# Seven products of block sums for the first MLP from token 768 on, its weights streamed from memory

## The chip, the cores and the metric

The program runs on one core of one Trainium2 chip. The metric is the device time of one execution in microseconds (us). The engines are named as the profile names them: PE (TensorE, matrix products), PEld (its weight loads), DVE (VectorE), ACT (ScalarE), POOL (GpSimd) and SP (SyncE, here the only queue that issues transfers).

## What is computed

The reference is windowed attention followed by two MLPs. There are 4 sequences of 576 tokens, 8 heads of 64, so 2304 tokens of width 512:

```
scores = q @ k.T / sqrt(64), masked: heads 0-3 see the 32 last positions,
         heads 4-7 every 4th of the 128 last positions
x  = softmax(scores) @ v                      # 2304 x 512
h  = x @ moe_w_in;   x  = relu(h)**2 @ moe_w_out      # 512 -> 2048 -> 512
h  = x @ moe2_w_in;  y  = silu(h)    @ moe2_w_out
```

The weights arrive as 64-bit floats. The kernel turns them into 32-bit values and splits each into a high and a low part; each product of the MLPs is made of three matmuls (high x high, high x low, low x high).

## The kernel before

**Order.** Nothing is scheduled by hand. Every piece of work is an `op` with the engines that may run it, a duration for each, its dependencies and a key. `Planner.order` builds the whole order before the launch: it takes again and again the operation that can start first (a key counts 0.005 us per unit, so keys only decide between near ties), and writes it to the program of its engine. A `gate` holds a transfer back until the first MLP or the second has come to a given key. One key unit stands for one 128-wide slice of the hidden layer on a 256-token tile. All transfers stand in one in-order queue, SP's.

**Buffers.** `POOLS` has 28 pages of 1024 words per partition ("u4"), 8 of 512 ("u2") and 2 of 512 ("u3"). `HOLDS` says which uses share a pool and `MOST` how many pages each use may hold. The converted first weights of MLP 1 (`w0`) hold 16 pages of u4, one for each of 16 slices, until the last token tile has used them. The second weights of the running MLP lie in 16 buffers of their own (`w1`).

**Attention.** 32 blocks: 8 halves of sequences (h, 288 tokens each) by 4 pairs of heads. A block is scores on PE, mask and row minimum on DVE (L572), exponential on ACT (L577), normalisation (L581 to L593), transpose (L600), product with v (L622), and then a cast into x's high part and a subtraction for its low part, for each 256-token tile that the block touches.

**First MLP** (`mlp`). Nine tiles of 256 tokens. The first three run interleaved, because their matmuls wait for weights that are still being converted and for attention; the other six follow one by one. For each slice c: S1 is 12 matmuls (L686 to L688), then max and square (L702, L710), cast and subtraction (L360, L367), then S2 is 12 matmuls (L734 to L736). The result goes to DRAM as `y1`.

**Second MLP** (`mlp2`). Four tiles of 512 tokens and one of 256. For a 512-token tile two slices (a pair) form a 2 x 2 block product, and S1 is done with seven products of block sums instead of eight: 42 matmuls of 256 columns for a pair (L832). Five additions put the blocks together (L846, L848). S2 has 24 matmuls of 512 columns for a pair (L881 to L883). The weights and their block sums are streamed for each tile from DRAM, where they were stored after conversion (`w2s`, `w2x`); `load_x2` reads `y1` back and makes the block sums of x (L799).

**Weights of the second MLP.** `weights(1, c, ...)` converts both halves of chunk c while MLP 1 runs, and stores them to `w2s`; `sums` makes block sums of the first half and stores them to `w2x`; `fetch` reads the second half back into `w1` during the last tile of MLP 1.

Of the kernel before, what the change touches and what calls it, by code (L numbers as in the profile page):

```python
# [23 lines left out]
P = 128  # L24
# [9 lines left out]
TILES = ([(t, 256) for t in range(0, NT, 256)], [(0, 512), (512, 512), (1024, 512), (1536, 512), (2048, 256)])  # L34

POOLS = {"u4": (28, 1024), "u2": (8, 512), "u3": (2, 512)}
HOLDS = {"w0": "u4", "wa": "u4", "ws": "u4", "wb": "u4", "wc": "u2", "h": "u4", "raw": "u4", "ap": "u4", "x": "u4", "x2": "u4", "g4": "u4", "st": "u4",
# [264 lines left out]
def c_dma(nbytes):  # L302
    return nbytes / 250e3
# [6 lines left out]
class Kern:  # L310
# [59 lines left out]
    def weights(self, m, c, key, dkey):  # L370
# [3 lines left out]
        for j in range(2):  # L374
            raw = self.spot("raw", n, I64)
            cv = self.spot("cv", n)
            both = (self.spot("st", 2 * n, F32R) if m else self.spot("w0", 2 * n, F32R) if j == 0 else
# [5 lines left out]
            k = key + (1.5 if m else 0.5) * j  # L383
# [3 lines left out]
                           [], dkey + (1.5 if m else 0.5) * j, [raw], name=f"R{at}")  # L387
            if m:
                load.gate = dkey + 1.5 * j
# [36 lines left out]
            if m:  # L426
                self.kept[c, j] = self.op({"DMA": c_dma(P * n * 8)}, lambda e, both=both, c=c, j=j: nc.sync.dma_start(
                    out=self.w2s[c, j], in_=both.tile.bitcast(F32)), [h, r], k, [], [both])
# [7 lines left out]
    def sums(self, f, key):  # L436

        nc = self.nc
        (ca, wa), (cb, wb) = self.cv[2 * f], self.cv[2 * f + 1]
# [7 lines left out]
        for i, (x, y, op) in enumerate(what):  # L447
# [5 lines left out]
                                + ([s[0]] if i == 3 else []), f"S{f}.{i}", True))  # L453
        self.kept[f, "s"] = []
        for i in range(2):
            hi, lo = Part(s[i], 0, PIECE), Part(s[i], PIECE, PIECE)
            h = self.op({"ACT": c_act(PIECE), "Pool": c_pool1(PIECE)}, lambda e, hi=hi, lo=lo: self.copy(
                e, hi.tile, self.f32(lo)), [done[2 * i], done[2 * i + 1]], key, [], [s[i]], f"h1.{f}.s{i}")
            deps = [h] + ([done[3]] if i == 0 else [])
            r = self.op({"DVE": c_dve(PIECE), "Pool": c_pool2(PIECE)}, lambda e, hi=hi, lo=lo: self.sub(  # L460
                e, lo.tile, self.f32(lo), hi.tile.bitcast(F32)), deps, key, [], [s[i]], f"l1.{f}.s{i}", True)
            self.kept[f, "s"].append(self.op({"DMA": c_dma(P * PIECE * 8)}, lambda e, i=i: nc.sync.dma_start(
                out=self.w2x[f, i], in_=s[i].tile.bitcast(F32)), [h, r], key, [], [s[i]]))
# [6 lines left out]
    def fetch(self, c, key):  # L470

        nc = self.nc
        both = self.buf("w1", NF, 2 * PIECE, F32R)
        o = self.op({"DMA": c_get(P * PIECE * 8)}, lambda e: nc.sync.dma_start(
            out=both.tile.bitcast(F32), in_=self.w2s[c, 1]), [self.kept[c, 1]], key, [both])
        o.gate = key
        self.wt[1, 1, c] = (Part(both, 0, PIECE), Part(both, PIECE, PIECE), o, o)

    def stream(self, f, key, whole):
# [4 lines left out]
        def load(use, src, n, deps, i):  # L484
            b = self.spot(use, n, F32R)
            o = self.op({"DMA": c_get(P * n * 4)}, lambda e: nc.sync.dma_start(
                out=b.tile.bitcast(F32), in_=src), deps, key + i, [b])
# [3 lines left out]
        b, o = load("wa", self.w2s[2 * f, 0], 1024, [self.kept[2 * f, 0]], 0)  # L491
        out["a11"], out["a12"] = [(Part(b, i, 256), Part(b, 512 + i, 256), o) for i in (0, 256)]
        n = 512 if whole else 1024
        b, o = load("wc" if whole else "wb", self.w2s[2 * f + 1, 0, :, :n], n, [self.kept[2 * f + 1, 0]], 0.1)
# [3 lines left out]
        else:  # L498
            for j in range(2):
                b, o = load("ws", self.w2x[f, j], 1024, [self.kept[f, "s"][j]], 0.2 + j)  # L500
# [28 lines left out]
    def attention(self, h, pair, key, step):  # L529
# [100 lines left out]
        for t in range(h * HALF // 256, (h * HALF + HALF - 1) // 256 + 1):  # L630
            lo, hi = max(h * HALF, t * 256), min(h * HALF + HALF, t * 256 + 256)
# [7 lines left out]
            def dst(b, t=t, lo=lo, hi=hi):  # L639
                o = b.tile[:, lo - t * 256:hi - t * 256]  # L640
                return o.rearrange("p (s r) -> p r s", r=DIL) if dil else o

            def src(lo=lo, hi=hi):
                if dil:
                    return xb.tile[:, :HALF].rearrange("p (r s) -> p r s", r=DIL)[
                        :, :, (lo - h * HALF) // DIL:(hi - h * HALF) // DIL]
                return xb.tile[:, lo - h * HALF:hi - h * HALF]

            w = hi - lo
# [104 lines left out]
    def load_x2(self, t, key):  # L754

        nc = self.nc
        t0, n = TILES[1][t]
        raw, got = [], []
        for j in range(2):
            b = self.buf("blk", BLK_BUFS, BLK_COLS)  # L760
            raw.append(b)
            for i in range(2):
                k = 2 * j + i
                deps = [self.ydone[0, u, k] for u, (u0, un) in enumerate(TILES[0]) if u0 < t0 + n and t0 < u0 + un]
                d = self.op({"DMA": c_dma(P * n * 4)}, lambda e, k=k, i=i, b=b: nc.sync.dma_start(
                    out=b.tile[:, n * i:n * i + n], in_=self.y1[k][:, t0:t0 + n]), deps, key + k, [] if i else [b], [b] if i else [])
                d.gate = key - 8
                got.append(d)
        x = self.x[1, t] = {}
# [5 lines left out]
        def keep(name, key, src, deps, uses):  # L775
# [5 lines left out]
                        [b], uses, f"xh{t}.{name}")  # L781
            r = self.op({"Pool": c_pool2(512), "DVE": c_dve(512)}, lambda e: self.sub(e, v(lo), src(), v(hi).bitcast(F32)),
                        [h], key + 0.1, [], uses + [b], f"xl{t}.{name}", True)
# [14 lines left out]
        for i, (p, q, uses, deps, of) in enumerate(what):  # L798
            done.append(self.op({"Pool": c_pool2(512), "DVE": c_dve(512)}, lambda e, i=i, p=p, q=q: self.eng[e].tensor_tensor(  # L799
                out=at(i), in0=p(), in1=q(), op=ALU.subtract), list(deps) + ([] if of is None else [done[of]]),  # L800
                key + 5 + i, [sums[i]], list(uses) + ([] if of is None else [sums[of]]), f"xs{t}.{i}", True))
            keep(("t1", "t2", "t4", "t3")[i], key + 5.5 + i, lambda i=i: at(i), [done[i]], [sums[i]])

    def mlp2(self, t, k0, fetched):

        nc = self.nc
        t0, n = TILES[1][t]
        x = self.x[1, t]
# [162 lines left out]


W_KEY = 4.0
A_LEAD = 22.0
B_LEAD = 6.0
A1 = -5.0
A2 = 6.0
# [93 lines left out]
```

## Time and profile before

| | |
|---|---|
| time, median of 3 runs | 919.78 us (919.67 to 920.01) |
| the profiled execution's own time | 919.36 us |
| its span, first to last instruction | 917.6 us |
| PE, PEld busy | 908.1 us (99%), 853.0 us (93%) |
| DVE, ACT, POOL busy | 588.1 us (64%), 466.6 us (51%), 66.9 us (7%) |
| transfers | 167.67 MB, 183 GB/s over the span |

The span is what the profile shows; the execution's time is 1.76 us longer. Busy shares are averages over stages that are limited by different things, so the rows further down are cut by stage. Matmuls overlap in the records (each is listed with 280 ns and more but the next starts after some 120 ns), so the pace is read from start to start.

### The profile page before, as it was taken

Reading aid. Unit: us, or ns where it says so; the run is one execution under the profiler, and the core shown is the slowest. Engines: PE = TensorE matmul, PEld = TensorE weight load, DVE = VectorE, ACT = ScalarE, POOL = GpSimd, SP = SyncE. Lnnn points to the kernel's source line nnn. Section 1 sums busy time; section 2 is a strip of 40 time slices with the busy share of each in tenths; the row PEclk is TensorE's granted clock in tenths of the full one; section 3 lists DMA queues with packets and bytes.
Section 4 is the critical chain, followed back from the end, with each engine's and each line's share of the span. In section 5 each row is a group of like instructions: output and inputs, shape, how many; then the busy total and the mean of one; then the engine's idle time right before and its main releaser. Section 6 shows DMA issues by size and latency. Waiting matters only on the chain.

```text
span 917.6 us, 19481 instructions
## 1 busy us (share of the span) xinstructions
PE 908.1 (99%) x7325; PEld 853.0 (93%) x7325; DVE 588.1 (64%) x1711; ACT 466.6 (51%) x1374; POOL 66.9 (7%) x83
## 2 busy tenths in 40 slices
PE   8999999999999999999999999999999999999998
PEld 7889999998999999999999999999999899999998
DVE  6999993478998988885522357466448454444422
ACT  7978772578877787775423234234224222322222
POOL 2224200001010111210000000000000000000000
PEclk9999999999999999999999999999999999999999
DMA  8356330147767586663004987556565657545150
GB/s 322 96 192 236 139 108 1 33 156 249 253 236 263 196 255 240 218 227 138 25 1 148 348 301 281 185 205 226 171 211 179 236 167 257 215 153 168 39 207 24
DMA packets 55390, 167.67 MB, mean 183 GB/s; under 512 B 6144, under 2 KB 12032, under 8 KB 55296
## 3 DMA queue, kind: packets, MB, share of 16 engines
q1 hardware_dynamic: 55296, 166.42, 52.7%
q8 instruction: 58, 0.95, 0.4%
q14 instruction: 36, 0.29, 0.1%
HBM read 131.79 MB, written 34.60 MB: 181 GB/s over the span
## 4 chain that ended last, share of the span: by engine, by line
PE 90%; DVE 5%; ACT 3%; issue 1%; POOL 0%; ACTq 0%; DVEq 0%
PE s L832 20%; PE s L686 7%; PE y L881 7%; PE y L882 7%; PE y L883 7%; PE s L688 7%; PE s L687 7%; PE y L734 7%; PE y L735 6%; PE y L736 6%; PE ax L550 2%; PE ax L622 1%; PE ax L600 1%; ACT ap L577 1%; DVE ap L593 1%; PE zx L734 1%
## 5 line engine op out<-in xcount | busy, mean ns | idle before, releaser
L686 PE MATMUL s<-x,w 128*128 128x256 f32 x576 | 166.2, 289 | 0.7 <-ACT ap L360 0.5
L688 PE MATMUL s<-x,w 128*128 128x256 f32 x576 | 162.7, 282 | 0.2 <-DVE w L367 0.2
L687 PE MATMUL s<-x,w 128*128 128x256 f32 x576 | 162.2, 282 | 0.0
L848 DVE TENSOR_TENSOR h<-s,h 128x512 f32<-128x512 f32 (+1 forms) x128 | 79.9, 624 | 113.3 <-PE s L832 112.0
L734 PE MATMUL y<-g,w 128*128 128x256 f32 x512 | 147.7, 289 | 0.0
L735 PE MATMUL y<-g,w 128*128 128x256 f32 x512 | 144.3, 282 | 0.1
L736 PE MATMUL y<-g,w 128*128 128x256 f32 x512 | 144.2, 282 | 0.0
L367 DVE TENSOR_TENSOR g<-r,g 128x256 fp32r<-128x256 f32 (+1 forms) x220 | 109.4, 509 | 36.2 <-ACT g L360 32.3
L360 ACT CAST g<-r 128x256 fp32r<-128x256 f32 (+1 forms) x224 | 103.6, 466 | 45.6 <-DVE r L710 27.2
L881 PE MATMUL y<-g,w 128*128 128x512 f32 (+1 forms) x320 | 118.0, 369 | 0.0
L882 PE MATMUL y<-g,w 128*128 128x512 f32 (+1 forms) x320 | 117.8, 368 | 0.0
L883 PE MATMUL y<-g,w 128*128 128x512 f32 (+1 forms) x320 | 117.7, 368 | 0.0
L710 DVE SCALAR_TENSOR_TENSOR r<-s,r 128x256 f32<-128x256 f32 x144 | 60.5, 420 | 86.8 <-ACT r L702 85.4
L686 PEld LDWEIGHTS s<-x,w 128*128 128x128 f32 x576 | 109.1, 189 | 4.4 <-ACT ap L360 0.7
L702 ACT ACTIVATE r<-s 128x256 f32<-128x256 f32 x144 | 54.7, 380 | 109.3 <-PE s L688 96.1
L688 PEld LDWEIGHTS s<-x,w 128*128 128x128 f32 x576 | 109.3, 190 | 0.5 <-DVE w L367 0.4
L687 PEld LDWEIGHTS s<-x,w 128*128 128x128 f32 x576 | 109.4, 190 | 0.0
L867 ACT ACTIVATE r<-h 128x512 f32<-128x512 f32 x64 | 37.0, 625 | 133.6 <-DVE h L848 133.6
L734 PEld LDWEIGHTS y<-g,w 128*128 128x128 f32 x512 | 96.8, 189 | 1.4
L832 PE MATMUL s<-x,ws 128*128 128x256 f32 x768 | 97.5, 283 | 0.0
L735 PEld LDWEIGHTS y<-g,w 128*128 128x128 f32 x512 | 96.6, 189 | 0.4 <-DVE g L367 0.3
L736 PEld LDWEIGHTS y<-g,w 128*128 128x128 f32 x512 | 96.4, 188 | 0.0
(90 smaller groups left out, 1610.8 us busy)
## 6 DMA issues: line engine op xcount, KB each, us to landing
raw<-w SPq DMA_DIRECT2D x64, 512.0 KB, 5.2
ws<-w2x SPq DMA_DIRECT2D x64, 512.0 KB, 4.4
wa<-w2s SPq DMA_DIRECT2D x40, 512.0 KB, 4.3
w2s<-st SPq DMA_DIRECT2D x32, 512.0 KB, 3.1
w2x<-st SPq DMA_DIRECT2D x16, 512.0 KB, 3.3
w<-w2s SPq DMA_DIRECT2D x16, 512.0 KB, 4.9
wc<-w2s SPq DMA_DIRECT2D x32, 256.0 KB, 4.6
blk<-qkv SPq DMA_DIRECT2D x8, 608.0 KB, 4.1
```

Of the source, the lines that this page charges most:

```text
L360: self.nc.scalar.copy(out=out, in_=in_)
L367: self.eng[eng].tensor_tensor(out=out, in0=a, in1=b, op=ALU.subtract)
L686: nc.tensor.matmul(o, wh.tile[:, s], xh, start=(kk == 0), stop=False)
L687: nc.tensor.matmul(o, wh.tile[:, s], xl, start=False, stop=False)
L688: nc.tensor.matmul(o, wl.tile[:, s], xh, start=False, stop=(kk == KC - 1))
L734: nc.tensor.matmul(o, wh.tile[:, s], gh.tile, start=(c == 0 and o0 == 0), stop=False, **kw)
L735: nc.tensor.matmul(o, wh.tile[:, s], gl.tile, start=False, stop=False, **kw)
L736: nc.tensor.matmul(o, wl.tile[:, s], gh.tile, start=False, stop=(c == NF - 1), **kw)
L832: nc.tensor.matmul(bank.tile[:, o:o + 256], wp, xp, start=i == 0, stop=last, skip_group_check=True)
L881: nc.tensor.matmul(o, wh.tile[:, s], gh.tile, start=c == 0, stop=False)
L882: nc.tensor.matmul(o, wh.tile[:, s], gl.tile, start=False, stop=False)
L883: nc.tensor.matmul(o, wl.tile[:, s], gh.tile, start=False, stop=(c == NF - 1))
```

## The change

Tiles of MLP 1 become 3 of 256 tokens and 3 of 512. The three large ones run through `mlp2`, which is generalised to both MLPs (for MLP 1 the two-step sigmoid product is replaced by one max-and-square instruction on DVE). Their first weights come by `stream(0, ...)` from DRAM: each converted chunk of `w0` is also stored (`w1s`), and `sums(f, key, 0)` adds high and low part of two chunks back together (`cw`), makes four block sums, splits and stores them (`w1x`). The attention output of tokens from 768 on is copied once (`xo`), stored to DRAM (`x1`), and read and split by `load_x`. The second half of MLP 2's weights is no longer converted during MLP 1's middle, stored and fetched: it is loaded and converted straight into `w1` during MLP 1's last tile. Keys, the transfer cost in the planner's table and a few hints move too.

```diff
-TILES = ([(t, 256) for t in range(0, NT, 256)], [(0, 512), ...
+TILES = ([(0, 256), (256, 256), (512, 256), (768, 512), (1280, 512), (1792, 512)], [(0, 512), ...
-    return nbytes / 250e3          # c_dma, the planner's cost of a transfer
+    return nbytes / 330e3
...
             else:
                 self.wt[m, j, c] = (hi, lo, h, r)
+                if m == j == 0:
+                    self.kept[0, c] = self.op({"DMA": ...}, ... nc.sync.dma_start(
+                        out=self.w1s[c], in_=both.tile.bitcast(F32)), [h, r], k + W1_BACK, [], [both])
...
+        if m == 0:                                   # sums
+            for c in (2 * f, 2 * f + 1):
+                b = self.spot("cw", PIECE)
+                wh, wl, h, l = self.wt[0, 0, c]
+                o = self.op({"Pool": ..., "DVE": ...}, ... tensor_tensor(out=b.tile, in0=wh, in1=wl, op=ALU.add) ...
-    def fetch(self, c, key):
...
-    def stream(self, f, key, whole):
+    def stream(self, m, f, key, whole):
+        if m == 0:
+            b, o = load("wc", src.rearrange("p (q a n) -> p q a n", q=2, a=2)[:, :, 1], 512, deps, 0.1, ...)
...
+            if t is None:                            # attention, tokens from 768 on
+                xo = self.spot("xo", w)
+                a = self.op({"ACT": c_actp(w), "DVE": c_dve(w)}, ... self.copy(e, place(xo.tile), src()) ...
+                self.kept[h, pair, "x"] = self.op({"DMA": c_dma(P * w * 4)}, ... out=self.x1[pair][:, lo:hi] ...
+                continue
...
-    def load_x2(self, t, key):
+    def load_x(self, m, t, key):
-    def mlp2(self, t, k0, fetched):
+    def mlp2(self, m, t, k0, fetched):
+                if m == 0:
+                    b = ... nc.vector.scalar_tensor_tensor(out=r.tile, in0=src(), scalar=0.0, in1=src(), op0=ALU.max, op1=ALU.mult)
...
+        for f in range(NF // 2):
+            self.sums(f, S1_FROM + S1_STEP * f, 0)
         for c in range(NF):
             k = W2_FROM + W2_STEP * c
-            self.weights(1, c, k, k - 4)
+            self.weights(1, c, k, k - 4, (0,))
...
-                    self.fetch(c, k + c)
+                    self.weights(1, c, k + 2 * c + 3, k + 2 * c - 1, (1,))
...
-A_LEAD = 22.0
+A_LEAD = 38.0
-W2_FROM = 66.0
-W2_STEP = 4.2
+S1_FROM = 27.44
+S1_STEP = 3.5
+W1_BACK = 40
+W2_FROM = 60.0
+W2_STEP = 6.0
```

`HINTS`, empty before, gets 16 entries: eleven shift a key by 1 to 16 units, two name ACT and three name POOL for one operation each.

## Rows read from the trace of the kernel before

**Rows 1.** The page's part 4, shares of the chain that ended last by engine

```profile
PE 90%; DVE 5%; ACT 3%; issue 1%; POOL 0%; ACTq 0%; DVEq 0%
```

**Rows 2.** Windows by stage: stretch and length, engines' busy us, PEclk, DMA share, GB/s

```profile
140.00:200.00 60.00, 60.00 (x508) 57.63 (x508) 27.34 (x116) 29.01 (x99) 0.65 (x1) 1.00 0.15 51
200.00:232.00 32.00, 30.09 (x281) 27.58 (x279) 27.38 (x107) 26.65 (x91) 3.41 (x4) 1.00 0.76 249
232.00:288.00 56.00, 55.77 (x543) 53.20 (x541) 51.88 (x194) 44.69 (x157) 6.70 (x9) 1.00 0.70 241
288.00:343.00 55.00, 54.68 (x522) 52.77 (x523) 47.71 (x173) 41.01 (x139) 6.12 (x7) 1.00 0.68 235
343.00:399.00 56.00, 56.00 (x534) 54.12 (x533) 47.93 (x171) 41.70 (x145) 9.53 (x11) 1.00 0.71 234
```

**Rows 3.** Windows of 20 us, same columns

```profile
20.00:40.00 20.00, 19.07 (x198) 15.52 (x197) 19.30 (x85) 18.35 (x68) 3.77 (x5) 1.00 0.34 110
40.00:60.00 20.00, 20.00 (x203) 18.00 (x200) 18.53 (x86) 17.15 (x67) 8.89 (x10) 1.00 0.55 189
...
320.00:340.00 20.00, 20.00 (x191) 19.26 (x190) 17.98 (x70) 15.23 (x51) 2.21 (x2) 1.00 0.81 264
...
500.00:520.00 20.00, 20.00 (x171) 20.00 (x170) 5.97 (x15) 5.53 (x14) 0.00 (x0) 1.00 0.97 365
```

**Rows 4.** Chain in order of time, second MLP: starts of S1, 512-token, then 256-token tile

```profile
642.56 5.03 PE s L832 x42
...
695.02 5.03 PE s L832 x42
...
888.46 2.87 PE s L832 x24
...
905.63 2.39 PE s L832 x20
```

**Rows 5.** Window over two pairs of a 512-token tile, columns as in Rows 2

```profile
640.86:661.85 20.99, 20.99 (x134) 19.07 (x133) 10.18 (x17) 5.42 (x10) 0.00 (x0) 1.00 0.54 176
```

**Rows 6.** DVE in order of time, back to back: start us, duration us, instruction

```profile
264.65 0.68 DVE L367 TENSOR_TENSOR st<-cv,st 128x512 fp32r<-128x512 f32 x1
265.25 0.42 DVE L710 SCALAR_TENSOR_TENSOR r<-s,r 128x256 f32<-128x256 f32 x1
265.58 0.68 DVE L414 CUSTOM_DVE_ANT_0 cv<-raw,cv 128x1024 uint16<-128x1024 uint16 x1
```

**Rows 7.** Groups by line on DVE, attention: busy us, mean ns | idle before

```profile
L572 DVE CUSTOM_DVE_ANT_0 ap<-ax,mask 96x128 f32<-96x128 f32 (+3 forms) x196 | 41.0, 256 | 8.9 <-PE ax L550 8.6
L593 DVE TENSOR_SCALAR ap<-ap,ast 96x128 f32<-96x128 f32 (+3 forms) x110 | 27.6, 293 | 0.5
L572 DVE DVE_READ_ACCUMULATOR2_ANT ast<- 72x1 f32 (+1 forms) x224 | 17.4, 78 | 0.0
L581 DVE TENSOR_SCALAR ast<-ast 72x4 f32<-72x4 f32 (+1 forms) x64 | 13.2, 208 | 5.3 <-ACT ap L577 5.1
L583 DVE RECIPROCAL ast<-ast 72x4 f32<-72x4 f32 (+1 forms) x64 | 10.5, 166 | 0.5
```

**Rows 8.** Instructions of one line: duration ns min/median/max, first and last start

```profile
L396 POOL TENSOR_SCALAR cv<-raw x33: 643/657/4674, 9.8 to 406.4; 128x512 f32<-128x512 f32 x33
L367 DVE TENSOR_TENSOR w<-cv,w x29: 673/681/692, 26.9 to 140.7; 128x512 fp32r<-128x512 f32 x29
```

**Rows 9.** SP in order of time: the 2nd and the 16th load of a later half's block

```profile
5.56 0.98 SPq L513 DMA_DIRECT2D blk<-qkv  x2
...
232.96 0.33 SPq L513 DMA_DIRECT2D blk<-qkv  x1
```

**Rows 10.** DMA issues: KB each, median us from issue to landing

```profile
ws<-w2x SPq DMA_DIRECT2D x64, 512.0 KB, 4.4
blk<-y SPq DMA_DIRECT2D x16, 256.0 KB, 3.9
y<-yo SPq DMA_DIRECT2D x36, 128.0 KB, 2.7
```

More of the change, by code (lines that the diff above doesn't have):

```diff
@@ L367, in sub, with weights @@
         self.eng[eng].tensor_tensor(out=out, in0=a, in1=b, op=ALU.subtract)
-    def weights(self, m, c, key, dkey):
+    def weights(self, m, c, key, dkey, js=(0, 1)):
         nc = self.nc
         n = PIECE
-        for j in range(2):
+        for j in js:
             raw = self.spot("raw", n, I64)
             cv = self.spot("cv", n)
-            both = (self.spot("st", 2 * n, F32R) if m else self.spot("w0", 2 * n, F32R) if j == 0 else
+            both = (self.spot("st", 2 * n, F32R) if m and not j else self.spot("w0", 2 * n, F32R) if j == 0 else
                     self.buf("w1", NF, 2 * n, F32R))
@@ L386, in weights @@
                            nc.sync.dma_start(out=raw.tile, in_=self.w[m][c, :, j, :]),
-                           [], dkey + (1.5 if m else 0.5) * j, [raw], name=f"R{at}")
+                           [], dkey + (0 if m else 0.5) * j, [raw], name=f"R{at}")
             if m:
-                load.gate = dkey + 1.5 * j
+                load.gate = dkey
             def top(e, cv=cv, pair=pair):
@@ L425, in weights @@
                 e, lv(), cs(), hv().bitcast(F32)), [h], k, [], [cv, both], "l" + at, True)
-            if m:
+            if m and not j:
                 self.kept[c, j] = self.op({"DMA": c_dma(P * n * 8)}, lambda e, both=both, c=c, j=j: nc.sync.dma_start(
-                    out=self.w2s[c, j], in_=both.tile.bitcast(F32)), [h, r], k, [], [both])
+                    out=self.w2s[c], in_=both.tile.bitcast(F32)), [h, r], k, [], [both])
                 if j == 0:
@@ L911, in run @@
         self.cv = {}
-        self.w2s = self.dr.tile([NF, 2, P, 2 * PIECE], F32, name="w2s")
+        self.w2s = self.dr.tile([NF, P, 2 * PIECE], F32, name="w2s")
+        self.w1s = self.dr.tile([NF, P, 2 * PIECE], F32, name="w1s")
+        self.w1x = self.dr.tile([NF // 2, 2, P, 2 * PIECE], F32, name="w1x")
+        self.x1 = [self.dr.tile([P, NT], F32, name=f"x1_{e}") for e in range(KC)]
         self.w2x = self.dr.tile([NF // 2, 2, P, 2 * PIECE], F32, name="w2x")
@@ L942, in run @@
         end = start(1, 0)
-        need = lambda h: max(t for t, (t0, n) in enumerate(TILES[0]) if t0 <= h * HALF + HALF - 1)
+        first = lambda h: next(t for t, (t0, n) in enumerate(TILES[0]) if t0 + n > h * HALF)
         for h, pair in blocks[NPAIR:]:
-            t = next(t for t, (t0, n) in enumerate(TILES[0]) if t0 + n > h * HALF)
+            t = first(h)
+            later = sum(first(g) == t for g in range(h + 1, NH))
             k = (A1 + A1S * pair if h == 1 else A2 + A2S * pair if h == 2 else
-                 start(0, t) - A_LEAD + A3S * pair)
+                 start(0, t) - A_LEAD + A3S * (pair - NPAIR * later))
             self.load_blk(h, pair, (B1 + 4 * pair) if h < 3 else k - B_LEAD)
@@ L978 @@
 A2S = 4.0
-A3S = 4.0
+A3S = 3.0
 B_LAG = 14.0
@@ L1002 @@
 V_LAG = 3
-HINTS = {}
+HINTS = {
+    "A5.0": ("", -8.0),
+    "B3.3": ("", -1.0),
+    "R0.4.0": ("", -4.0),
+    "gl0.0.10": ("Pool", 0),
+    "gl0.5.3.1": ("Pool", 0),
+    "h0.14.1": ("", -1.0),
+    "n7.3.0.1": ("", 2.0),
+    "n7.3.1.3": ("ACT", 0),
+    "p0.3.3.1": ("", -1.0),
+    "t0.0.1.0": ("", -8.0),
+    "v0.15.1": ("ACT", 0),
+    "xh0.4.b21": ("", 16.0),
+    "xh1.3.t2": ("", -2.0),
+    "xs0.4.3": ("Pool", 0),
+    "z0.11.1": ("", 16.0),
+    "z0.3.1": ("", 4.0),
+}
 @with_exitstack
```

147 lines of the change are left out of this document (87 added, 60 removed).

## The prediction

> **What bounds the kernel now.** I read the chain that ended last first: nine tenths of it is PE [rows 1]. Then the windows by stage, for a mean over the span says little here. From 140 us to the end PE is busy in practically every microsecond; between 200 and 399 us it stands for only 1.91, 0.23, 0.32 and 0 us in the four stretches [rows 2]. So from there on the time is the number of matmul columns, and whatever takes columns away shortens the kernel as long as nobody else makes PE wait. The others are not idle, though: DVE is full for 85.6% of 200 to 232 us and for 147.5 of the 167 us from 232 to 399, that is 88% [rows 2]. DMA runs at about 237 GB/s there with its engines 70% busy. Behind that lies a calm part: at 500 to 520 us DVE needs 5.97 of 20 us [rows 3]. The change moves work into both.
>
> **What it removes: PE.** The second MLP shows both ways of doing a tile in the steady state. In a 512-token tile S1 of a pair starts at 642.56 and, five pairs on, at 695.02: 10.49 us for a pair, 8 pairs are 83.9 us. In its 256-token tile a group of 24 + 24 matmuls of 256 columns repeats three times from 888.46 to 905.63: 5.72 us, 8 of them 45.8 us [rows 4]. MLP 1's 256-token tile has the same 384 matmuls. Two such tiles are 91.6 us, so each pair of tiles that becomes one gains 7.6 us, three of them 22.9 us. Of that 17.2 us are the 144 matmuls left out (0.119 us each by the same rows), the rest is that S2 takes 512 columns at once. Attention's matmuls stay the same, only earlier. So without any wait the span is 917.6 - 22.9 = 894.7 us, and with the 1.76 us that lie around the span the time is 896.5 us.
>
> **What it adds, part one: the opening, until the first large tile.** From instruction to instruction DVE takes 0.60 us for 512 columns and 0.33 for 256 [rows 6]. New sums of w_in: for a pair two additions of 512, four of 256, two subtractions of 512, 3.7 us, eight pairs 29.8 us. New for the large tile's x: seven subtractions and four differences of 512, 6.6 us. Attention of two more blocks: the sixteenth load of a later block is issued at 232.96 [rows 9] with two buffers, so about 14 are done when the three first tiles end, and all 16 must be; a block costs DVE 3.4 us (109.7 us of its five largest groups over 32 blocks [rows 7]), so 7 us. Gone from here: subtractions of x for eight blocks (some 0.7 us each, 5.6) and the second halves of the early chunks of the other MLP's weights (about 6 us). Net 31.8 us. The cover is the hole from 140 to 232 us, where DVE is idle for 32.7 + 4.6 = 37.3 us [rows 2]. It fits, with 5.5 us to spare. I cost it at nothing because of a second cover: the last weights of MLP 1 are converted at 140.7 us [rows 8], while PE still has matmuls of the three first tiles until about 232; a conversion that comes some us later finds PE busy with the other two tiles. Only four of the eight pairs of sums are due before the large tile is under way. If that cover were gone, each us of DVE too much would be one of PE.
>
> **Part two: the three large tiles.** They last 3 x 83.9 us plus PE's share of attention for the last three halves: a stretch with one 256-token tile and about four blocks takes 55.5 us (the last two of [rows 2]), less 45.8, so 2.4 us a block, 12 blocks 29 us; in all 281 us. DVE's work in it: two pairs cost 10.18 us [rows 5], so 40.7 us a tile, 122 in all; x for two further tiles and the other MLP's first one, 11 operations of 0.60 each, 20; twelve blocks of attention 41; 13 of 16 chunks of the first half of w2 (0.33 + 3 x 0.60 = 2.1 us to convert, and 1.3 us for sums) 45; 16 chunks of its second half 34. Sum 262 us, 93% of 281. DVE is above its 88% of today, and PE's idle time grows with it. Bounds: at 88% PE lost 0.55 us of 167 [rows 2], by which 281 us lose 0.9; at 85.6%, from 200 to 232, with bursts of loads, 1.91 of 32, which would be 16.8. The row nearest in load is 20 to 60 us: DVE 37.8 of 40 us, 95%, PE loses 0.93 [rows 3], by which it is 6.5 us. The load forecast, 93%, lies between the stretch at 88% and this one; the middle of their two prices is 3.7, I take 4 us and keep 0.9 and 16.8 as ends. ACT is not a limit: for MLP 1's tiles it gives up one read of PSUM per slice, and it was busy for 41 of 55 us.
>
> POOL is no way out. Its one-operand multiply takes 0.66 us at the median but once 4.67 us [rows 8]. [...]
>
> **DMA.** A chunk is 512 KB, 0.524 MB [rows 10]. A pair streams one wa, two ws and half a chunk of wc, 1.835 MB; 24 pairs 44.0 MB. With the second half of w2 (8.4), 13 chunks of the first half with two stores each (20.4), x stores and loads (4.9), blocks of q, k and v (6.4) and y (3.7) the three tiles move 87.8 MB in 281 us, 313 GB/s. Today's mixed stretches move 237 at 70% busy, which is 339 at full; loads alone reached 365 at 0.97 [rows 3]. So DMA has 7 to 17% left. Streams are asked for three pairs ahead, 31 us, against 4.4 us to landing [rows 10], so queueing of some us is hidden. What is behind a waiting transfer on SP matters more: stores of converted weights wait there for DVE, and the next stream stands behind them. In the opening, 17 MB of new stores (w1s, w1x) fall on 140 to 200 us, where DMA is 15% busy. Price: 0.
>
> **Sum.** 896.5 + 4 = 900.5 us. The profiled execution was at 919.36 and the median is 919.78, so the difference between the two (0.42) is within what I can tell.
>
> **Rivals.**
>
> A. *DVE becomes the bound in the large tiles.* If its order cannot be packed closer than the 88.3% of today, 262 us of work take 297 us: 16 us too much, 912.5 us. For it: 93% on average means single tiles above it. The last one has 40.7 + 6.6 + 34 us and the rest of the first half in 83.9 us. Against it: those 34 us are due only in the following tile, which leaves half of DVE free (10.18 of 21 us [rows 5]). [...] 17 in 100.
>
> B. *DMA becomes the bound, and the kernel is slower.* Place: the large tiles. Break-even: the gain is gone when 87.8 MB take 281 + 22.9 us, at 289 GB/s. The highest mixed stretch of today is 264 GB/s at 0.81 busy [rows 3]; if loads and stores mixed do no better than that, they take 332 us, 51 too many, and the time is 948. For it: mixed stretches never showed more, and the in-order queue idles at each wait. Against it: at 264 the engines had a fifth of their time free, and nothing asked for more. 8 in 100.
>
> C. *The first large tile starts late.* Its x makes a trip through DRAM: after the last block a copy, a store (2.7 us), a load (3.9 us [rows 10]) and the splits, some 12 us. If that block stays where it is today (233 plus some 14 us [rows 9]), the tile starts near 259 instead of 237, and PE has nothing else: 22 us lost, 918.5, no change. Against it: the gate of these blocks is moved 28 to 32 units earlier, and the hole at 140 us has room. 7 in 100.
>
> **Chances and range.** My forecast, PE bound with up to some 9 us of waits (895.5 to 906): 68 in 100. A reaches from 906 to about 917, with a tail above. A measurement of this kernel can tell about 0.2%, 1.84 us, from no change. Faster than that: all of the forecast, 16 of A's 17, 2 of C's: 0.86. Same: 1 of A and 3 of C, 0.04. Slower: B's 8 and 2 of C, 0.10. The range for 8 in 10 goes from 895, just under the sum without any wait, to 914, a little above the price of A. The forecast's own range is 895.5 to 906.
>
> **What the profile after would show.** Right: starts of S1 in MLP 1's large tiles 10.5 us apart (12 to 13 where attention runs between), PE idle for under 9 us from 200 us on, DVE near 93% up to the end of MLP 1 and over 60% in the first tile of MLP 2, DMA over 300 GB/s for long stretches, the hole at 140 to 200 us filled. A would show PE waiting for g or h with DVE at 100%. B would show PE's weight loads waiting for wa, ws or wc. C would show one hole of 10 to 20 us before the first large tile. The prediction is wrong if PE's pace in the new S1 is not that of the second MLP, or if waits add up to more than 17 us.

## The result and the profile after

| | before | after |
|---|---|---|
| time, median (range) | 919.81 us (919.67 to 920.01) | 908.88 us (905.33 to 910.31, 4 executions) |
| the profiled execution | 919.36 us, span 917.6 | 909.49 us, span 907.7 |
| ratio after to before | | 0.9875, 95% interval 0.9846 to 0.9904 |

The change gains 10.9 us where 19.3 were forecast (900.5 us). The time lies in the stated range, and above the 906 up to which the forecast itself should reach. The four executions are not alike: the one with a mean granted clock of 1.00 took 905.33 us, the three at 0.998 took 908.28 to 910.31.

The chain that ended last, shares by engine, answers to [rows 1]: PE has fallen from 90% to 74%, and what replaced it is VectorE, ScalarE and DMA.

```profile
PE 74%; DVE 14%; ACT 6%; DMA 4%; issue 2%; SPq 0%; POOL 0%; ACTq 0%; DVEq 0%; POOLq 0%
```

Windows of the kernel after, columns as in [rows 2], which they answer together with [rows 3]:

```profile
80.00:140.00 60.00, 58.34 (x531) 54.49 (x530) 57.29 (x195) 49.65 (x158) 12.75 (x13) 1.00 0.72 241
140.00:200.00 60.00, 57.48 (x545) 53.75 (x546) 59.19 (x215) 44.82 (x152) 10.37 (x13) 1.00 0.64 231
200.00:240.00 40.00, 38.56 (x356) 36.76 (x354) 29.96 (x99) 28.38 (x90) 4.04 (x5) 1.00 0.83 278
240.00:300.00 60.00, 57.48 (x484) 50.54 (x483) 49.89 (x177) 37.67 (x132) 4.93 (x9) 1.00 0.90 321
300.00:365.00 65.00, 64.72 (x466) 56.41 (x465) 55.00 (x165) 38.31 (x114) 4.74 (x5) 1.00 0.91 312
365.00:430.00 65.00, 65.00 (x426) 59.03 (x424) 51.29 (x87) 22.47 (x41) 4.42 (x5) 1.00 0.85 301
430.00:500.00 70.00, 70.00 (x445) 63.72 (x444) 64.59 (x112) 33.44 (x61) 6.02 (x7) 1.00 0.89 323
500.00:520.00 20.00, 18.01 (x106) 16.00 (x105) 19.89 (x37) 11.63 (x21) 1.80 (x2) 0.91 0.93 361
520.00:560.00 40.00, 40.00 (x249) 36.17 (x249) 32.34 (x55) 20.25 (x37) 1.81 (x2) 1.00 0.64 230
```

First see that the hole of [rows 2] at 140 to 200 us is gone: VectorE went from 27.34 to 59.19 of 60 us. Then see where PE stands. Between 80 and 300 us it is idle for 1.66 + 2.52 + 1.44 + 2.52 = 8.1 us, where the kernel before lost 2.5 in the same 220 us: nothing up to 200 us (its row from 80 us on follows, the next is in [rows 2]), then 2.5. From 300 to 500 us the kernel after loses 0.28. Then come 1.99 us in one stretch of 20 us, and in that row alone PEclk is below 1.00.

```profile
80.00:140.00 60.00, 60.00 (x546) 59.45 (x546) 58.83 (x148) 43.88 (x109) 12.02 (x9) 1.00 0.43 150
```

The large tiles run at the pace of the second MLP. The chain in order of time (start, duration, instruction) shows S1 of the pairs:

```profile
376.65 5.03 PE s L859 x42
...
429.11 5.03 PE s L859 x42
...
502.57 5.03 PE s L859 x42
```

376.65 to 429.11 are five pairs in 52.46 us, 10.49 each, the figure of [rows 4]; 502.57 is seven pairs later, 10.49 each again.

DMA issues (KB each, median us from issue to landing), which answer to [rows 10]:

```profile
raw<-w SPq DMA_DIRECT2D x64, 512.0 KB, 7.2
ws<-w2x SPq DMA_DIRECT2D x64, 512.0 KB, 4.7
ws<-w1x SPq DMA_DIRECT2D x48, 512.0 KB, 6.6
```

The load of unconverted weights, raw<-w, took 5.2 us at the median in the kernel before:

```profile
raw<-w SPq DMA_DIRECT2D x64, 512.0 KB, 5.2
```

Most of the difference lies in the large tiles: from 238 to 520 us the median is 7.3 us after against 4.5 before, up to 240 us it is 7.0 against 6.4.

**A balance of PE.** Busy time hides short waits, since matmuls overlap in the records (in the kernel after, just before 510 us, one of 512 columns is listed with 0.39 us, and the next starts after 0.23). So I took the starts of all matmuls of a trace, subtracted from each start-to-start gap the median gap of that shape, and added up what is left over ("lost"). The filler matmuls of the opening (they multiply a constant tile and their results are not used) and the useful rest are the other two parts of the span:

```
us            lost: 0-80  80-240  240-380  380-540  sum   filler  rest   span
before               8.8    10.8      5.0      0.1  24.6    30.4  862.6  917.6
after                8.2    18.1      8.1      3.9  38.3    28.1  841.3  907.7
```

Columns saved: 21.3 us. Filler saved: 2.3. Given back in waits: 13.7, of which 7.4 from 80 to 240 us, 3.1 from 240 to 380, and 3.8 near 510. These sizes depend on how finely shapes are told apart: by partitions, columns and type alone, the same sum gives 7.8, 4.3 and 4.8 us for the three stretches and 26.4 for the columns. The opening and the place near 510 are two different things, and they need two sets of experiments.

**The opening: many short waits.** Waits of PE from 80 to 300 us, by line and releaser (us in total, times, longest), kernel after:

```profile
PE s L711 <- DVE ast L585: 1.5, 1, 1.5
PE s L711 <- DVE r L735: 1.3, 3, 0.6
PE ax L635 <- DVE ast L585: 1.0, 1, 1.0
PE ax L613 <- ACT ap L360: 0.9, 2, 0.7
...
```

There are eleven such rows and no single wait above 1.5 us; attention's steps (ast, ap, xo) and the MLP's own (r, g, h) take turns. One example of how such a wait comes about, from the chain in order of time:

```profile
237.84 7.02 DMA raw<-w
244.94 0.52 ACT cv L394
245.52 0.66 ACT raw L402
246.18 0.54 ACT ap L604 x2
246.72 1.98 ACT ap L590 x11
...
250.91 0.56 ACT xo L360
251.52 0.45 PE ax L613 x3
```

A load of unconverted weights takes 7.02 us. ScalarE's next instructions in its fixed order convert it, and it stands idle for 0.47 us until the load is there. Behind the conversion come normalisation and exponential of attention (L604, L590) and a copy (xo), and PE's transposes at 251.52 wait 0.58 us for that copy. Matmuls of the large tile (L859) stand behind the transposes in PE's order. So the late load is one part of such a wait, and the work that stands in front of the operand on ScalarE is the other.

**The stop at 510 us.** PE, then ScalarE, then VectorE in order of time (start, duration, instruction, idle time before it):

```profile
509.95 0.39 PE L915 MATMUL y<-g,w 128*128 128x512 f32 x1
512.33 1.57 PE L859 MATMUL s<-x,wa 128*128 128x256 f32 x6 [1.99 <-issue]
513.70 0.63 PE L913 MATMUL y<-g,w 128*128 128x512 f32 x1
514.12 0.63 PE L914 MATMUL y<-g,w 128*128 128x512 f32 x1
```

```profile
511.34 0.62 ACT L360 CAST g<-r 128x512 fp32r<-128x512 f32 x1 [0.59 <-DVE r L895]
511.86 0.36 ACT L873 COPY h<-s 128x256 f32<-128x256 f32 x1
```

```profile
509.36 0.68 DVE L414 CUSTOM_DVE_ANT_0 cv<-raw,cv 128x1024 uint16<-128x1024 uint16 x1
509.96 0.69 DVE L367 TENSOR_TENSOR x<-stg,x 128x512 fp32r<-128x512 f32 x1
510.57 0.68 DVE L895 SCALAR_TENSOR_TENSOR r<-h 128x512 f32<-128x512 f32 x1
```

PE's six matmuls at 512.33 follow the copy L873, which clears a bank of S1. The profile names only "issue" for this wait; that the copy ends it is my reading of the order. The copy stands behind a cast (L360) in ScalarE's order, the cast waits 0.59 us for L895, and L895 stands in VectorE's queue behind a conversion of the last weights and a subtraction of the other MLP's x, without a gap. After the pause, up to 515.82 us, the matmuls of 512 columns start 0.42 us apart instead of 0.23, and the granted clock from 512.33 to 515.82 is 0.51. The pause of 1.99 us and this stretch together cost 3.8 by the balance.

### The profile page after: what moved, and what is told of

The parts are those of the page before. It is cut to its first block, busy times and chain, and to the rows that moved or that the text cites. A ratio compares the mean times of both kernels' runs of the same rounds, so it can differ in the third digit from the quotient of the medians.

```text
span 907.7 us, 18193 instructions
## 1 busy us (share of the span) xinstructions
PE 888.2 (98%) x6589; PEld 806.3 (89%) x6589; DVE 662.7 (73%) x1749; ACT 455.0 (50%) x1260; POOL 78.9 (9%) x97
## 4 chain that ended last, share of the span: by engine, by line
PE 74%; DVE 14%; ACT 6%; DMA 4%; issue 2%; SPq 0%; POOL 0%; ACTq 0%; DVEq 0%; POOLq 0%
PE s L859 32%; PE y L913 12%; PE y L914 12%; PE y L915 12%; ACT ap L590 2%; DMA raw<-w 2%; DVE st L367 1%; ACT ap L604 1%; PE ax L961 1%; DVE st L466 1%; DVE g L367 1%; DVE ap L585 1%; DVE ap L606 1%; DVE r L735 1%; DMA x<-xo 1%
## 5 line engine op out<-in xcount | busy, mean ns | idle before, releaser
L875 DVE TENSOR_TENSOR h<-s,h 128x512 f32<-128x512 f32 x224 | 139.5, 623 | 135.2 <-PE s L859 121.7
L913 PE MATMUL y<-g,w 128*128 128x512 f32 (+1 forms) x512 | 194.5, 380 | 0.0
L914 PE MATMUL y<-g,w 128*128 128x512 f32 (+1 forms) x512 | 193.2, 377 | 0.0
L915 PE MATMUL y<-g,w 128*128 128x512 f32 (+1 forms) x512 | 192.8, 377 | 0.0
L859 PE MATMUL s<-x,ws 128*128 128x256 f32 x1344 | 172.4, 283 | 0.7 <-DVE ap L362 0.6
L859 PEld LDWEIGHTS s<-x,ws 128*128 128x128 f32 x1344 | 166.0, 192 | 1.4 <-DVE ap L362 0.7
L360 ACT CAST g<-r 128x512 fp32r<-128x512 f32 (+1 forms) x176 | 94.2, 542 | 58.5 <-DVE r L895 29.0
L367 DVE TENSOR_TENSOR g<-r,g 128x512 fp32r<-128x512 f32 (+1 forms) x170 | 99.5, 605 | 13.8 <-ACT g L360 10.2
L859 PE MATMUL s<-x,wa 128*128 128x256 f32 x768 | 105.0, 285 | 2.0 <-issue 2.0
L859 PEld LDWEIGHTS s<-x,wa 128*128 128x128 f32 x768 | 100.8, 192 | 6.7 <-issue 2.4
L590 ACT ACTIVATE ap<-ap,ast 96x128 f32<-96x128 f32 (+3 forms) x224 | 82.6, 372 | 17.7 <-DVE ast L585 17.6
L711 PE MATMUL s<-x,w 128*128 128x256 f32 x192 | 56.7, 295 | 3.0 <-DVE ast L585 1.5
L873 ACT COPY h<-s 128x256 f32<-128x256 f32 x56 | 20.7, 370 | 74.5 <-PE s L859 73.1
L713 PE MATMUL s<-x,w 128*128 128x256 f32 x192 | 54.4, 284 | 0.7 <-DVE w L367 0.7
L712 PE MATMUL s<-x,w 128*128 128x256 f32 x192 | 54.1, 282 | 0.0
L859 PE MATMUL s<-x,wc 128*128 128x256 f32 x336 | 49.3, 282 | 0.0
```

Of the source, the lines that this page charges most:

```text
L360: self.nc.scalar.copy(out=out, in_=in_)
L367: self.eng[eng].tensor_tensor(out=out, in0=a, in1=b, op=ALU.subtract)
L590: es.append(self.op({"ACT": c_act(nk) + 0.185}, lambda e, i=i, n=n, c=c, p=p, st=st: nc.scalar.activation(out=p.tile[:n, c], in_=p.tile[:n ...
L711: nc.tensor.matmul(o, wh.tile[:, s], xh, start=(kk == 0), stop=False)
L712: nc.tensor.matmul(o, wh.tile[:, s], xl, start=False, stop=False)
L713: nc.tensor.matmul(o, wl.tile[:, s], xh, start=False, stop=(kk == KC - 1))
```

## The experiments

Unless a diff moves something, the order of the instructions is that of the kernel after. Ratios are against the kernel before on the same chip. The kernel after has 0.9875 (0.9846 to 0.9904), so a ratio whose interval overlaps that one does not show a gain over it. Each kernel has one profile; its lost time is that of one execution.

**1. The opening: one load at a time.** The block sums of w_in are not computed:

```diff
-  lambda e, ...: self.eng[e].tensor_tensor(out=b.tile, in0=wh, in1=wl, op=ALU.add)   # sums, m == 0
+  lambda e: None
-  ... tensor_tensor(out=self.f32(part[i]), ...); copy(hi); sub(lo)
+  m and ...
```

> The order and all transfers stay as in the changed kernel, but the block sums of w_in are not computed: the two additions, four block sums, two casts and two subtractions of each of the eight pairs are left out (about 30 us of DVE work and 10 us of ACT work in the first 240 us), and the stores to w1x carry another tile, so the output is not the reference's. Theory A (VectorE is full in the opening, and PE's many short waits there come from it): PE's idle time between 80 and 240 us, 7.5 us, falls by 4 to 7 us, and the time falls from 908.9 to 902 to 905. Theory D (the waits there are the chains of the attention that was moved into the opening, each link of it on another engine): the time falls by 2 us or less, since those chains stay.

907.71 us, 0.9857 (0.9836 to 0.9879). VectorE fell from 59.19 to 41.57 us in 140 to 200, and yet PE lost more there (55.83 busy against 57.48). From 80 to 240 us PE stands for 6.5 us, in the kernel after for 5.6 by the same windows (not 7.5, as the expectation has it). VectorE's amount of work alone isn't what holds PE up: up to 140 us PE loses 0.02 us and not 1.66, and it waits later.

The stores of the converted first weights, one of 32 kept:

```diff
-  nc.sync.dma_start(out=self.w1s[c], in_=both)        # and the two of w1x
+  c or nc.sync.dma_start(out=self.w1s, in_=both)      # all streams read this one
```

> The order and all engine work stay as in the changed kernel, but of the 32 stores of converted first weights and of their block sums (w1s, w1x) only one is issued, and the streams of the large tiles all read that one, so 16.3 MB of stores and 31 entries of the queue are gone from the opening; the output is not the reference's. Theory B (queue): PE's idle time from 80 to 240 us falls by 4 us or more, time 902 to 905. Theory A (VectorE): it falls by less than 1.5 us, 907 to 909.

908.05 us, 0.9862 (0.9838 to 0.9885). DMA falls to 90 GB/s from 140 to 200 us; PE's waits stay (4.9 us from 80 to 240 against 5.6).

The loads for the later attention blocks, cut to 96 columns, into two buffers that are kept:

```diff
-  nc.sync.dma_start(out=b.tile[:, :n], in_=src)
+  m = 96 if len(two) > 2 and h > 2 else n            # two: the buffers in use
+  nc.sync.dma_start(out=b.tile[:, :m], in_=src[:, :m])
```

> The order of all instructions stays. The loads of q, k and v of the attention blocks from the fourth half of a sequence on bring 96 of some 1,200 columns, into two buffers that are kept, so the data of those blocks is stale; everything else is done. Theory D1 (the short waits of the opening come from block loads that land late, 4 us and more behind other transfers): the loss of TensorE between 80 and 300 us, 8.1 us in the changed kernel, falls below 4, and the time to about 904. Theory D2 (the waits come from the links between engines, each a little late in a fixed order): the loss stays above 6.5 us and the time within 2 us of 908.9.

905.36 us, 0.9843 (0.9823 to 0.9862); PE's loss from 80 to 300 us is 6.1 us, between what the two theories asked for. The median is 3.5 us lower, with overlapping intervals, and the stop near 510 is still there (18.11 of 20 us).

**2. The opening: all at once.** The three edits together, and in those blocks exponential and normalisation on 8 columns:

> The order of all instructions stays. Left out together: the block sums of w_in (VectorE and ScalarE), 15 of the 16 stores of the converted first weights, 11 to 12 of every 12 columns of the late attention blocks' loads, and in those blocks the exponential and the normalisation work on 8 columns of 72 to 128. Each of the first two alone moved the time by 1.2 us at most. If the opening has several limits of about the same length, each hidden by the next (theory D3): removed together, TensorE's loss between 80 and 300 us falls from 8.1 to under 3.5 us, and the time to 902 to 904. If it is the order itself, waits between engines that no shorter work removes (D2): the loss stays above 5 us and the time above 905.

(Of the stores, this one leaves out only those of w1s.) 898.62 us, 0.9772 (0.9753 to 0.9792). The loss from 80 to 300 us is 4.0 us: less than the order alone (D2) would leave, more than D3's 3.5, and the time is shorter than either theory had it. Then the same without the thinner softmax, that is sums, w1s stores and block loads:

> The order of all instructions stays. As e6_opening_freed (no block sums of w_in, 1 of 16 stores of the converted first weights, short loads for the late attention blocks), but the softmax of those blocks at full width. Theory D3 (several limits of about the same length in the opening: sums, transfers and block loads together): as there, TensorE's loss from 80 to 300 us about 4 us and the time within 2 us of 898.6. Theory D2' (the chain of softmax steps through ScalarE is what TensorE waits for there, the other three only stand beside it): the loss is back above 5.5 us, and the time 902 to 905. ScalarE's share of the thinner softmax is at most 0.2 us for each of some 200 instructions.

900.44 us, 0.9788 (0.9770 to 0.9806), within the 2 us of D3. The loss from 80 to 300 us is 5.4 us, between D3's 4 and the 5.5 of D2', so it decides for neither. Windows of this kernel:

```profile
80.00:140.00 60.00, 59.94 (x552) 56.65 (x551) 47.75 (x182) 49.21 (x162) 13.46 (x14) 1.00 0.44 139
140.00:200.00 60.00, 58.20 (x566) 55.59 (x564) 43.78 (x179) 41.75 (x148) 4.32 (x8) 1.00 0.47 164
200.00:240.00 40.00, 38.20 (x362) 35.65 (x360) 29.93 (x117) 28.15 (x95) 3.85 (x6) 1.00 0.81 270
240.00:300.00 60.00, 58.23 (x466) 51.60 (x467) 47.43 (x149) 34.09 (x115) 4.60 (x9) 1.00 0.83 284
```

The medians of the three edits are lower by 1.2, 0.8 (with the w1x stores) and 3.5 us one by one, 5.5 in sum, and by 8.4 together. Only the last is clear of the spread of the kernel after. The lost time by the same balance; the last two rows are the kernels with thinner and with later last conversions of experiment 3, whose order and work up to 425 us are those of the kernel after:

```
us                  80-240  240-380  380-540
before                10.8      5.0      0.1
after                 18.1      8.1      3.9
no sums               16.2     11.8      4.6
no stores             16.3     11.1      4.9
short loads           15.9      8.0      3.8
all three             13.6      7.3      2.7
and thin softmax      12.3      7.0      2.0
thin last             15.9      9.0      0.1
last later            16.9     11.2      0.5
```

The last two rows show how much one and the same opening varies from profile to profile: 15.9 to 18.1 us before 240 us and 8.1 to 11.2 behind. Each edit alone (15.9 to 16.3) lies inside that, so the 2 us that it seems to free are not shown; nor is what the first two seem to give back by 380, where a PEclk of 0.97 from 240 to 300 us stands in both and in "last later" too. The three edits together lie below the spread and bring back 4.5 of the 7.3 us before 240 us and 0.8 of the 3.1 behind; 1.2 us of their 8.4 are lost time near 510. So the work and the transfers that the change brought into the opening do cost PE time there, and the theory of the fixed order alone (a loss above 5 us and a time above 905 with everything freed) falls. That the parts hide each other is likely, but with this spread it is not shown that the single gains fall short of the joint one. The thinner softmax gives 1.8 us more, with overlapping intervals; from 80 to 300 us ScalarE is busy for 10.9 us less with it (142.3 against 153.2), some 0.05 us for each of the 200 instructions, where the expectation allows 0.2.

**3. The stop at 510 us.** The last tile's conversions nearly free for VectorE (8 of 512 columns, and the low part made by ScalarE):

```diff
+  n8 = slice(0, 8) if m and j else slice(None)
-  nc.vector.tensor_scalar(out=vi(), in0=vi(), scalar1=3, ...)
+  nc.vector.tensor_scalar(out=vi()[:, n8], in0=vi()[:, n8], scalar1=3, ...)
...                                                     # sign and addition likewise
+  nc.scalar.copy(out=lv(), in_=cs()) if last else self.sub(...)
```

> The order and all transfers stay as in the changed kernel, but in the conversion of the second half of the other MLP's weights (the last large tile) the shift, the sign and the addition touch 8 columns in place of 512, and the low part is a copy on ACT, so DVE has about 34 us less to do between 430 and 540 us and the output is not the reference's. Theory A (VectorE): the stop of 2 us at 510 us and the stretch at half clock behind it, together 3.8 us, are gone, time 904.5 to 906. Theory B (transfers: the loads that ran at 418 GB/s just before): the stop stays, 908 to 910.

905.2 us, 0.9843 (0.9822 to 0.9865), and in the profile the stop is gone while transfers stay high (0.86, 315 GB/s):

```profile
500.00:520.00 20.00, 20.00 (x126) 18.08 (x125) 13.82 (x34) 13.58 (x24) 0.69 (x1) 1.00 0.86 315
```

Then the other side, transfers without touching VectorE:

```diff
-  nc.sync.dma_start(out=self.w2s[c], in_=both)         # and the two of w2x
+  c or nc.sync.dma_start(out=self.w2s, in_=both)       # all streams read this one
```

> The order of all instructions stays. Left out: 15 of the 16 stores of MLP 2's converted first halves and all stores of their block sums (some 13.6 MB of the 88 MB that the large tiles move); MLP 2 streams the one stored chunk every time, so its output is not the reference's. Theory T (in the large tiles a load of unconverted weights comes some 3 us late because the transfers are close to full; ScalarE and VectorE wait for it in their fixed order, with work behind it that TensorE needs): loads of w land in about 5 us instead of 7, TensorE's loss from 240 to 365 us falls from 2.8 to under 1.5 us, and the stop near 510 us, where 361 GB/s move, gets under 1 us; 903 to 905. Rival (VectorE's full queue alone, transfers do not matter): the loss stays above 2.3 us and the stop stays; 907 to 910.

904.38 us, 0.9839 (0.9824 to 0.9854). The stop is gone here too, with VectorE as full as before (19.64 of 20 us). What changed is how long ScalarE waits for unconverted weights from 200 to 520 us, first in the kernel after, then here:

```profile
ACT cv L394 <- DMA raw<-w: 23.8, 10, 5.3
```

```profile
ACT cv L394 <- DMA raw<-w: 5.5, 5, 1.9
```

So by these profiles the stop needs both, weights that land late and a VectorE with no room to catch up; taking away either was enough in the one profile of each, while the three single edits of the opening, which touch neither, left 3.8 to 4.9 us of lost time there. Two other parts of the expectation missed. Loads of unconverted weights landed in 6.2 us from 238 to 520 us, not in about 5 (7.3 in the kernel after). And from 240 to 365 us PE lost 3.2 us, not less than the 2.8 of the kernel after; what it waits for there stays open.

The conversions moved later, all work done:

```diff
-  self.weights(1, c, k + 2 * c + 3, k + 2 * c - 1, (1,))
+  self.weights(1, c, k + 2 * c + 11, k + 2 * c + 7, (1,))
```

> Correct kernel. One edit: the conversions of the last second weights, in the last tile of MLP 1, get keys 8 units later (start plus 11 instead of plus 3), so more of them fall into the first tile of MLP 2, where VectorE has room. Theory A for the last tile (VectorE is full there, its queue delays the copy that frees a bank, TensorE pauses for 2 us and then runs at half clock): no stop near 510 us, 3 to 4 us less, 905 to 906. Rival: the weights then come too late for the first products of MLP 2 that need them, and a wait of some us appears after 530 us: 908 or more.

907.16 us, 0.9859 (0.9840 to 0.9878), between the two theories. From 500 to 520 us PE is busy for 20.00 us, and from 520 to 560 us for 39.85 of 40, so neither the stop nor the rival's wait is there. But this profile lost 3.4 us from 240 to 300 us, a stretch whose order the edit leaves as it was, with PEclk 0.83 in ten of them; against the kernel after the gain can't be told from none.

**4. Without "straight into place".** The second half of MLP 2's weights is converted in the middle of MLP 1, stored and fetched, as before the change, with the large tiles kept:

```diff
-  self.weights(1, c, k, k - 4, (0,))
+  self.weights(1, c, k, k - 4)                          # both halves, stores to w2s[c, j]
...
-  self.weights(1, c, k + 2 * c + 3, k + 2 * c - 1, (1,))
+  self.fetch(c, k + 2 * c)
```

> Correct kernel, one part of the change undone: the second half of MLP 2's weights is converted in the middle of MLP 1 together with the first half, stored and fetched in the last tile, as before the change; the large tiles stay. Theory A' (VectorE is close to full in the large tiles, 262 of 281 us in the forecast, so work moved forward by 34 us there must push something that TensorE needs): PE waits of 5 to 15 us between 240 and 480 us, 914 to 924. Rival (the large tiles have room; only the last tile is full): 905 to 910, with the stop near 510 us gone.

931.14 us, 1.0122 (1.0103 to 1.0141): slower than the kernel before, by more than either theory had it. Windows of this kernel, then waits of PE from 240 to 560 us:

```profile
300.00:365.00 65.00, 62.37 (x454) 55.18 (x453) 60.04 (x148) 37.16 (x97) 3.33 (x5) 1.00 0.92 329
365.00:430.00 65.00, 60.93 (x378) 53.68 (x377) 49.21 (x115) 30.01 (x73) 1.45 (x2) 0.92 0.89 316
430.00:500.00 70.00, 64.30 (x375) 56.77 (x374) 51.20 (x89) 26.83 (x50) 1.92 (x2) 0.93 0.90 324
```

```profile
PE s L868 <- ACT h L882: 4.3, 3, 2.9
PE y L922 <- ACT yo L360: 3.1, 2, 1.9
```

By its busy time VectorE isn't the bound: from 365 to 500 us it works 100.4 of 135 us. Transfers are busy throughout, 316 to 329 GB/s with a share of about 0.9 in each of these stretches. And PE waits neither for wa nor for ws, but most of all for the copy out of a bank (h, yo); on the chain there stand loads of unconverted weights of 6 to 8 us and conversions behind them. Against the kernel after this one moves 16.8 MB more (16 chunks stored and 16 fetched) and needs 22 us more. That the transfers are the bound is argued from this and not shown: no run took transfers away from this kernel. Another reading is open. Its loads of unconverted weights land in 7.0 us from 238 to 520 us, no later than the 7.3 of the kernel after, but from 240 to 500 us the transfer queue stands much longer at stores that wait for VectorE's last step of a conversion, here first, then in the kernel after:

```profile
SPq L427 <- DVE st L367: 51.3, 13, 7.5
```

```profile
SPq L427 <- DVE st L367: 18.4, 6, 6.7
```

All transfers stand in this one queue, and what comes behind such a store is issued after it: in the kernel after the one at 430.79 us had waited for 6.7 us, and the load of wa behind it was issued at 431.21.

**5. Constants.** The hints taken out (`HINTS = {}`):

> All work of the changed kernel, with the 16 hints taken out, so only the order and three subtractions on GpSimd differ. If the waits are set by how much VectorE has to do (theory A), the time stays within 3 us of 908.9. If they are set by the fine order that the hints chose (a third theory, C), it becomes 5 us or more slower.

911.27 us, 0.9907 (0.9870 to 0.9944): perhaps 2 us, the intervals overlap, and within the 3 us of theory A. The planner's price of a transfer:

```diff
-    return nbytes / 330e3          # c_dma
+    return nbytes / 290e3
```

> Correct kernel. One edit: the planner's price of a transfer is 290 GB/s instead of 330 (before the change it was 250), so that the order is built for transfers that take 14% longer; the stretch from 200 to 300 us moves 278 to 321 GB/s. Theory T: an order with later loads allowed for has fewer waits for late loads, 903 to 907. Rival (the order is no better, since the planner gives up something else for it): 908 to 913.

912.66 us, 0.9931 (0.9917 to 0.9946): an order that allows for longer transfers is worse. PE's waits turn up elsewhere, 2.98 us from 300 to 365, 2.09 from 500 to 520 and 2.30 from 520 to 560. Then that price with attention and the first halves 4 key units earlier and the last halves 4 later:

```diff
-A_LEAD = 38.0
+A_LEAD = 42.0
-W2_FROM = 60.0
+W2_FROM = 56.0
-  self.weights(1, c, k + 2 * c + 3, k + 2 * c - 1, (1,))
+  self.weights(1, c, k + 2 * c + 7, k + 2 * c + 3, (1,))
```

> Correct kernel. Four constants: the price of a transfer 290 GB/s instead of 330, attention 4 key units earlier (lead 42), the first conversions of MLP 2's weights 4 units earlier (from 56), those of the last second weights 4 units later. Theory T with the full VectorE of the last tile: fewer waits in the opening and no stop near 510 us, 901 to 905. Rival (the losses are what an order of this density costs, and each move only shifts them): 906 to 910.

908.13 us, 0.9890 (0.9872 to 0.9908). The stop is gone (20.00 of 20 us from 500 on), and the opening lost 7.8 us of PE from 80 to 300. The rival's time holds: in these two kernels moving work about shifted the losses. None of the kernels that do all the work is measurably faster than the change itself.

## Why the forecast was 9 us too low

That the time lies in the stated range is partly luck. It missed the forecast's own range (895.5 to 906) and lies where rival A was priced (906 to about 917), and A is not what happened.

The forecast's span was 898.7 us (900.5 less the 1.8 around it), the measured one is 907.7. By the balance the 9.0 us fall on its terms so:

```
term                          forecast   measured   difference
PE columns                      -22.9      -21.3       +1.6
filler matmuls                    0         -2.3       -2.3
opening, 0 to 240 us              0         +6.8       +6.8
waits in the large tiles         +4         +6.9       +2.9
```

The opening's 6.8 us are those of one profile; the two others of the same opening give 3.7 and 4.9 (lost 23.2 and 24.5 us up to 240 us, 19.6 before). The median of all executions is 8.4 us above the forecast.

**PE's columns: right.** The pace of 10.49 us for a pair is exactly that of [rows 4], and the 22.9 us lie between the 21.3 and 26.4 of the two ways to tell shapes apart.

**The opening at nothing: the step that failed.** Its first cover, the idle VectorE of [rows 2], was there and was filled to the brim (59.19 of 60 us). The second cover was the mistake: "a conversion that comes some us later finds PE busy with the other two tiles". The order is fixed before the launch. PE can't take what is ready; it stands at its next instruction, as at 251 us for 0.58 us, with other matmuls behind it. Nor was VectorE the only thing to count. The change brought sums, stores, and block loads and softmax of more attention into the same 200 us: sums, stores and loads taken out together gave 8.4 us. How much of it is each one's is open, since one by one (0.8 to 3.5 us) they can't be told from the spread.

**The waits in the large tiles: 4 us, measured 6.9.** Inside the ends I gave (0.9 and 16.8), but not for the reason of the term. VectorE was to be at 93%; it worked 241.5 of the 282 us from 238 to 520, 86%. Its attention shows 64 masks in that time, at seven for a block nine blocks and not twelve, so more of it fell into the opening. What cost 3.8 us was one place where, by experiment 3, late weights and a full VectorE met: a pause of 1.99 us, and behind it 3.49 us at a granted clock of 0.51.

**Transfers at a price of 0: half right.** The amount was right (318 GB/s over the 282 us against 313 forecast), and that streams asked for three pairs ahead hide the queueing is right as well: from 230 us on no wait of PE or of its weight loads is for wa, ws or wc. The step missed the other loads. Unconverted weights land 2 us later than before, in the large tiles 2.8, and what stands behind them on ScalarE and VectorE is work that PE needs.

**Rivals.** A (VectorE becomes the bound, 912.5): no, 86%. C (x's trip through DRAM): no; S1 of the first large tile starts at 237.9 us, before the small tiles' last S2. B (transfers become the bound, slower): not in this kernel. It had put mixed traffic at 264 GB/s by [rows 3]; the kernel after moves 318. With 16.8 MB more the rate from 240 to 500 us rises only from 314 to 323 and the time goes to 931, which looks like B and is not proven to be it (experiment 4). The part of the change that I treated as a side issue, weights converted straight into place, is what keeps the kernel out of that state.

**The signs I named.** The 10.5 us, the idle time under 9 us from 200 us on (1.44 + 2.52 + 0.28 + 1.99 = 6.2), VectorE above 60% in the first tile of MLP 2 (32.34 of 40 us from 520 to 560 and 20.77 of the next 40, 66%) and DMA above 300 GB/s are all there; VectorE near 93% up to the end of MLP 1 is not (86%). None of them looked at PE's waits from 80 to 200 us, where the largest part of the loss was (15.4 us by the balance, 5.4 before). That POOL is no way out rests on one multiply of 4.67 us among 33 [rows 8], and no run here shows it.

**Open.** How far the spread of 905 to 910 us between executions of one kernel is the clock after the stop alone: the one execution at 1.00 was 3 us faster than the next, about what the stop costs, but only the profiled one has a trace.

## What to carry to other kernels

In a program with a fixed order, a backlog on the busiest engine is no cover: a late operand stops it at that instruction, as it stopped PE at 251 us for 0.58 us with matmuls behind. When work is moved into an idle stretch, count for every engine and every queue how full it becomes, and expect losses to turn up elsewhere when the order is changed. When the transfers are busy for nine tenths of a stretch (0.89 from 238 to 520 us here, where raw<-w landed in 7.3 us, against 4.5 at 0.56 before), look for the loads that are not prefetched far ahead, and at what stands behind their consumers. Before an edit's effect on one stretch is read from one profile, see how far profiles of an unchanged stretch differ; here it was 2 to 3 us.

## What the runs showed of the hardware

In the kernel after, a PE pause of 1.99 us was followed by a granted clock of 0.51 from 512.33 to 515.82 us, with 512-column matmuls 0.42 us apart instead of 0.23; of the 3.8 us that the place cost by the balance, 1.8 lie behind the pause. With the short block loads PE stood for 1.89 of the 20 us from 500 on, and the granted clock there was 0.91. It isn't a sure thing: with the opening freed (all three edits) PE stood for 1.87 of the same 20 us, and the granted clock was 1.00.

Transfers moved 420 GB/s from 505 to 510 us and 318 on the mean from 238 to 520 us; over those 282 us loads of 512 KB took 6.3 (wa<-w1s), 6.7 (ws<-w1x) and 7.3 us (raw<-w) at the median to land. In the same stretch of the kernel before, at 192 GB/s, raw took 4.5.

```profile
505.00:510.00 5.00, 5.00 (x34) 4.50 (x32) 5.00 (x10) 2.79 (x5) 0.00 (x0) 1.00 1.03 420
510.00:515.50 5.50, 3.51 (x13) 2.82 (x12) 5.50 (x12) 3.38 (x7) 0.00 (x0) 0.72 0.73 255
```
